# Linear attention feeding a gated feed-forward layer: q laid out transposed by the host, one piece per partition for k, v and w_in, and another order of the first batch's stages

## The chip, the cores and the metric

The kernel runs on one core of one Trainium2 chip. The metric is the device time of one execution in microseconds (us). A smaller time is better. Laying the inputs out on the host, before the launch, is not part of the time.

## What is computed

For each of 8 batches and 8 heads (sequence 576, head size 64) the kernel forms `kv = k^T v` (64 by 64), then `out = q kv`, divides each row of `out` by its root mean square and multiplies it by `g_norm`. The heads side by side give a token's 512 values, for 4608 tokens. A feed-forward layer follows:

```python
kv = np.einsum('bhsd,bhse->bhde', k, v)
out = np.einsum('bhsd,bhde->bhse', q, kv)
rms = np.sqrt(np.mean(out * out, axis=-1, keepdims=True) + 1e-06)
x = (out / rms * g_norm)            # heads side by side: 4608 tokens x 512
h = x @ w_in                        # 512 x 2048
g = h * (1.0 / (1.0 + np.exp(-h)))
return g @ w_out                    # 2048 x 512
```

All data are 32-bit. The weights arrive as 64-bit numbers in the program's view, two 32-bit words each, that the kernel turns into a 32-bit value itself.

## The kernel before, in words

**The feed-forward part.** Tokens are taken in 9 tiles (`t`) of 512, the 2048 hidden values in 16 blocks (`f`) of 128. One step is one `(t, f)`. Every product is made of three matmuls, since each factor is split into a rounded high part and the rest (low part): `products` (L503) writes 12 matmuls of 512 columns into a PSUM bank `hp`, `gate` (L512) makes `gh`, `gf` and `gl` of it, and `project` (L532), two steps later (`LAG`), adds 12 matmuls of 512 columns into four banks `acc`.

**The weights.** A block of `w_in` or `w_out` is loaded by `load_block` (L95) and prepared once, in the first tile: `bits` (L125) makes the 32-bit value on VectorE, five instructions for the first blocks and three for later ones, whose first two are `magnitude` (L115) on ScalarE and GpSimd; `split_block` (L163) rounds on ScalarE (L166) and subtracts on GpSimd (L167).

**Attention of batches 1 to 7.** Class `Pair` treats two heads at once (4 pairs per batch), spread over the steps of the feed-forward part by `plan` (L551): `mm_kv` (L246), `split_kv` (L253 to L257), `turn_q` (L261, a transposition of 32x32 blocks on VectorE), `split_q` (L266 and L267), `mm_out` in two halves (L277 to L279), then the norm and `to_tile` (L312, L313), which writes the tiles `xh` and `xl` that the products read. Here q is loaded in four DMAs per pair, in runs of 32 values (128 bytes), and k and v in two DMAs each.

**Attention of batch 0.** It has to be done before the first products. Class `FirstPair` loads q, k and v of a pair into buffers (`early`) that weights will need later. `turn_q` (L341) transposes q by TensorE, `copy_q` (L346) brings it back from PSUM on ScalarE (once on VectorE); `make_kv` (L352) and `copy_kv` (L359) give the two 64x64 blocks; `make_out` (L365) multiplies; `square` (L369) and `norm` (L442 to L448) make the norm on VectorE, with one square root on ScalarE (L446); `make_x` (L378) transposes the result, and `x_from` writes the x tile, for pairs 0 and 1 by ScalarE twice and GpSimd (L467 to L469), for pairs 2 and 3 by ScalarE and VectorE (L458, L459). Class `Rest` does the last 64 tokens of the batch for all pairs.

**What sets the order.** Nothing is scheduled by a planner: each engine executes its instructions in the order in which the Python code issues them, and waits in that order. `ORDER` (L26) is the order of the loads, all on SyncE's queue, where from the ninth DMA on each issue waits until the one eight places earlier has landed. Lines 630 to 689 are the first batch's stages; the loop from L700 on is the rest.

## Time and profile before

| what | value |
|---|---|
| three timed runs | 891.77, 892.54, 892.55 us; median 892.54 |
| the profiled execution | 893.95 us, span 892.1 us |
| TensorE (PE) busy | 871.0 us, 98% of the span |
| VectorE (DVE) busy | 337.7 us, 38% |
| ScalarE (ACT) busy | 307.5 us, 34% |
| GpSimd (POOL) busy | 176.8 us, 20% |
| DMA | 108,389 packets, 55.26 MB; 76,464 packets under 512 bytes |

The profiled execution took 893.95 us; the profile covers 892.1 us of it (the span), and 1.85 us lie around it. Times in the profile count from the span's start. An instruction's row has its start, its duration, its engine, line and operation, and in brackets how long the engine stood idle before it and what released it.

### The profile page before, as it was taken

The page shows a single profiled execution, that of the slowest core. Times are in us where ns is not written, and L with a number is a line of the kernel's source. Part 1 is how long each engine was busy: PE and PEld are TensorE (multiplying, and loading weights), DVE is VectorE, ACT ScalarE, POOL GpSimd, SP SyncE. Part 2 cuts the span into 40 slices and gives each one's busy share as a digit, 9 for nine tenths or more (in the row PEclk, how much of TensorE's full clock was granted, in tenths as well). Part 3 has the DMA queues.
Part 4 walks back from the last instruction along what each step waited for, and adds up shares of the span by engine and source line. Part 5 has one row for each costly group of instructions (what it writes and reads, how often), then busy time and mean ns, then how long its engine had stood idle before and what let it go on. Part 6 is the DMA issues. An engine that isn't in the chain of part 4 may idle for free.

```text
span 892.1 us, 11345 instructions
## 1 busy us (share of the span) xinstructions
PE 871.0 (98%) x4438; PEld 713.1 (80%) x4438; DVE 337.7 (38%) x617; ACT 307.5 (34%) x684; POOL 176.8 (20%) x172
## 2 busy tenths in 40 slices
PE   7879989999999999999999999999999999999998
PEld 6658868888888888888888888888888888888887
DVE  5888894233232423341433233332523141111111
ACT  4567634332343224322432243322432231112121
POOL 1489963101120002101210112010310020000000
PEclk9899989999999999999999999999999999999999
DMA  9869402310052004300431024100400010001001
GB/s 243 257 212 326 117 0 80 87 41 1 11 148 49 0 1 128 80 1 1 116 65 28 1 71 96 41 1 1 127 1 1 1 47 1 1 1 48 0 1 48
DMA packets 108389, 55.26 MB, mean 62 GB/s; under 512 B 76464, under 2 KB 101808, under 8 KB 108336
## 3 DMA queue, kind: packets, MB, share of 16 engines
q1 hardware_dynamic: 108336, 54.54, 22.5%
q8 instruction: 35, 0.57, 0.3%
q14 instruction: 18, 0.15, 0.1%
HBM read 45.09 MB, written 9.44 MB: 61 GB/s over the span
## 4 chain that ended last, share of the span: by engine, by line
PE 87%; DMA 3%; DVE 3%; POOL 3%; issue 2%; SPq 1%; ACT 0%; DVEq 0%; POOLq 0%
PE hp L507 41%; PE acc L537 40%; PE at L246 2%; DMA early_wo<-in_q 1%; DMA wi<-in_moe_w_in 1%; DMA wo<-in_moe_w_out 1%; POOL wi L167 1%; PE at L278 1%; PE at L279 1%; PE at L277 1%; POOL full L120 1%; PE at L537 1%; DMA kv<-in_k 1%; DVE m L476 1%; POOL wo L167 1%
## 5 line engine op out<-in xcount | busy, mean ns | idle before, releaser
L507 PE MATMUL hp<-xh,wi 128*128 128x512 f32 x1144 | 355.4, 392 | 2.1 <-POOL wi L167 2.1
L537 PE MATMUL acc<-wo,gh 128*128 128x512 f32 (+1 forms) x1152 | 355.3, 390 | 1.4 <-POOL wo L167 1.4
L518 DVE TENSOR_TENSOR gl<-gf,gh 128x512 fp32r<-128x512 f32 x128 | 88.6, 692 | 500.5 <-ACT gf L517 500.5
L507 PEld LDWEIGHTS hp<-xh,wi 128*128 128x128 f32 x1144 | 215.9, 189 | 46.0 <-POOL wi L167 3.2
L537 PEld LDWEIGHTS acc<-wo,gh 128*128 128x128 f32 x1152 | 214.8, 188 | 45.8 <-POOL wo L167 1.8
L507 PE MATMUL hp<-xl,wi 128*128 128x512 f32 x572 | 227.8, 398 | 3.5 <-ACT wi L166 3.5
L516 ACT ACTIVATE gh<-hp 128x512 fp32r<-128x512 f32 x143 | 85.5, 598 | 416.8 <-PE hp L507 416.6
L537 PE MATMUL acc<-wo,gl 128*128 128x512 f32 x576 | 222.5, 386 | 0.0
L507 PEld LDWEIGHTS hp<-xl,wi 128*128 128x128 f32 x572 | 108.0, 189 | 26.8 <-ACT wi L166 3.9
L537 PEld LDWEIGHTS acc<-wo,gl 128*128 128x128 f32 x576 | 108.2, 188 | 23.8
L313 POOL TENSOR_TENSOR xl<-o,xh 128x448 fp32r<-128x448 f32 (+7 forms) x56 | 53.2, 951 | 343.5 <-ACT xh L312 343.5
L517 ACT ACTIVATE gf<-hp 128x512 f32<-128x512 f32 x143 | 84.6, 592 | 0.0
L267 POOL TENSOR_TENSOR ql<-qT,qh 128x576 fp32r<-128x576 f32 x28 | 40.1, 1431 | 177.0 <-ACT qh L266 88.5
L283 ACT ACTIVATE sq<-at 128x288 f32<-128x288 f32 x56 | 23.2, 415 | 39.4 <-PE at L279 26.8
L253 ACT COPY kvm<-at 64x64 f32<-64x64 f32 x56 | 11.6, 207 | 59.4 <-PE at L246 59.1
L304 DVE SCALAR_TENSOR_TENSOR o<-o,gcol,yT 128x448 f32<-128x448 f32 (+7 forms) x56 | 31.2, 557 | 2.0
L246 PEld LDWEIGHTS at<-kv 128*64 128x64 f32 (+1 forms) x560 | 20.8, 136 | 12.0 <-issue 9.7
L246 PE MATMUL at<-kv 128*64 128x64 f32 (+1 forms) x560 | 26.5, 231 | 0.0
L312 ACT CAST xh<-o 128x448 fp32r<-128x448 f32 (+7 forms) x56 | 24.8, 442 | 5.0 <-DVE o L304 5.0
L297 DVE STREAM_TRANSPOSE yT<-y 128x448 f32<-128x448 f32 (+7 forms) x56 | 25.9, 463 | 0.0
L167 POOL TENSOR_TENSOR wi<-full,wi 128x512 fp32r<-128x512 f32 x16 | 21.4, 1334 | 21.2 <-ACT wi L166 21.2
L284 ACT COPY o<-at 128x288 f32<-128x288 f32 x56 | 22.7, 406 | 4.0 <-POOL xl L313 4.0
(104 smaller groups left out, 514.5 us busy)
## 6 DMA issues: line engine op xcount, KB each, us to landing
out<-ob SPq DMA_DIRECT2D x35, 256.0 KB, 2.1
wi<-in_moe_w_in SPq DMA_DIRECT2D x16, 512.0 KB, 6.4
wo<-in_moe_w_out SPq DMA_DIRECT2D x16, 512.0 KB, 11.1
qt<-in_q SPq DMA_DIRECT2D x112, 72.0 KB, 3.7
kv<-in_k SPq DMA_DIRECT2D x28, 256.0 KB, 3.1
kv<-in_v SPq DMA_DIRECT2D x28, 256.0 KB, 3.6
kv<-in_k SPq DMA_DIRECT2D x28, 32.0 KB
kv<-in_v SPq DMA_DIRECT2D x28, 32.0 KB
```

What stands on the lines that cost most here:

```text
L167: nc.gpsimd.tensor_tensor(out=w[:, 1, :], in0=full, in1=w[:, 0, :].bitcast(F32), op=ALU.subtract)
L246: nc.tensor.matmul(out=self.kv[h], lhsT=self.k[rows, c, :], rhs=self.v[rows, c, :], start=(r == 0), stop=(r == 4))
L267: nc.gpsimd.tensor_tensor(out=self.ql, in0=self.qT, in1=self.qh.bitcast(F32), op=ALU.subtract)
L297: nc.vector.transpose(out=self.yT.rearrange("p (j a) -> p j a", a=32), in_=y[:, a // 32:e // 32].unsqueeze(2).to_broadcast([P, (e - a) // ...
L304: nc.vector.scalar_tensor_tensor(out=self.o[:, a:e], in0=self.o[:, a:e], scalar=gcol, in1=self.yT, op0=ALU.mult, op1=ALU.mult)
L312: nc.scalar.copy(out=th[:, self.c, w], in_=self.o[:, a:e])
L313: nc.gpsimd.tensor_tensor(out=tl[:, self.c, w], in0=self.o[:, a:e], in1=th[:, self.c, w].bitcast(F32), op=ALU.subtract)
L507: nc.tensor.matmul(out=hp[:, :TN], lhsT=w[:, a, fs], rhs=x[:, c, :], start=(c == 0 and i == 0), stop=(c == NP - 1 and i == 2),)
L516: nc.scalar.activation(out=gh, in_=hp[:, :TN], func=AF.Silu)
L517: nc.scalar.activation(out=gf, in_=hp[:, :TN], func=AF.Silu)
L518: (nc.gpsimd if t == 0 else nc.vector).tensor_tensor(out=gl, in0=gf, in1=gh.bitcast(F32), op=ALU.subtract)
L537: nc.tensor.matmul(out=bank, lhsT=g[:, ns], rhs=w[:, a, cs], start=(f == 0 and i == 0), stop=(f == NF - 1 and i == 2))
```

## The change

- On the host, `lay_out` gives q as [batch, pair, 128 (head and its 64 values), 576 tokens], k and v as [batch, pair, 128 partitions, 576 values], and `w_in` as 16 blocks of [128 partitions, 512 values]. So each load of q, k, v or a block of `w_in` is one DMA with one contiguous piece per partition: 2,304 bytes for q, k and v, 4,096 for `w_in`.
- q is ready for the matmuls when it lands. The transpositions of q (L261 on VectorE, L341 and L399 on TensorE) and their copies (L346, L406) are gone. `q` itself takes the place of `qT`.
- `FirstPair` uses the `Pair` code for its load and for k^T v: 10 matmuls over 128 rows in place of 12 over 96, into an `h` bank of its own for each pair.
- The loads of the first batch come in another order, and `w_in`'s block 1 behind the third pair.
- The first batch's stages are in another order: `b1`'s conversion moves behind the norm of pair 1, `make_x` of pairs 0 and 1 moves forward, the first six products come in another order.
- In tile 0 the tokens keep their order, so the x tile of batch 0 is written along PSUM's order.

```diff
 ORDER = """
-    wi0 q0 kv0 wi1 q1 kv1 q2 kv2 q3 kv3 g wi2 qq wo0 wi3 wo1 wi4 wo2 b0 wi5 wo3 b1 wi6 wo4 wi7 wo5 b2
+    wi0 p0 g p1 p2 wi1 p3 wi2 wo0 wi3 wo1 wi4 wo2 b0 wi5 wo3 b1 wi6 wo4 wi7 wo5 b2
     wi8 wo6 wi9 wo7 b3 wi10 wo8 wi11 wo9 wi12 wo10 wi13 wo11 wi14 wo12 wi15 wo13 wo14 wo15
...
+        src = w_in.bitcast(I32)[f] if kind == "wi" else w_out.bitcast(I32)[f * P:(f + 1) * P, :]
+        nc.sync.dma_start(out=t.rearrange("p a b -> p (a b)"), in_=src)
...
+        def load(self, place=None):
+            self.k, self.v, self.q = (
+                place() if place else kvq.tile([P, S], F32, name=name, tag="kvq") for name in ("k", "v", "q")
+            )
+            for t, src in ((self.k, k), (self.v, v), (self.q, q)):
+                nc.sync.dma_start(out=t, in_=src[self.b, self.c])
...
-        def turn_q(self):
-            self.qT = tmp.tile([P, S], F32, name="qT", tag="tmp")
-            nc.vector.transpose(out=self.qT, in_=self.q)
...
-            nc.scalar.copy(out=self.qh, in_=self.qT)
-            nc.gpsimd.tensor_tensor(out=self.ql, in0=self.qT, in1=self.qh.bitcast(F32), op=ALU.subtract)
+            nc.scalar.copy(out=self.qh, in_=self.q)
+            nc.gpsimd.tensor_tensor(out=self.ql, in0=self.q, in1=self.qh.bitcast(F32), op=ALU.subtract)
...
         b0, b1, b2 = (bits("wi", f) for f in range(3))
-        p0.turn_q()
-        p0.copy_q([nc.scalar.copy] * 2)
+        run(b0)
         p0.make_kv()
         p0.copy_kv()
-        run(b0)
+        split("wi", 0)
         p0.make_out()
-        split("wi", 0)
-        run(b1)
-        p1.turn_q()
         p0.square()
-        p1.copy_q([nc.scalar.copy] * 2)
         p1.make_kv()
+        p1.copy_kv()
         norm(p0)
-        p1.copy_kv()
-        p2.turn_q()
         p1.make_out()
         p1.square()
-        p2.copy_q([nc.scalar.copy, nc.vector.tensor_copy])
+        nc.vector.tensor_scalar(out=gcol, in0=gcol, scalar1=float(D) ** 0.5, scalar2=None, op0=ALU.mult)
         p2.make_kv()
+        make_x(p0)
         p2.copy_kv()
         norm(p1)
-        nc.vector.tensor_scalar(out=gcol, in0=gcol, scalar1=float(D) ** 0.5, scalar2=None, op0=ALU.mult)
-        p3.turn_q()
         p2.make_out()
-        p3.copy_q([nc.scalar.copy] * 2)
         p2.square()
-        split("wi", 1)
+        run(b1)
         p3.make_kv()
+        make_x(p1)
         p3.copy_kv()
-        norm(p2, b2[:2])
-        make_x(p0)
+        norm(p2)
         p3.make_out()
         p3.square()
-        norm(p3, b2[2:3])
-        run(b2[3:])
-        make_x(p1)
+        split("wi", 1)
         make_x(p2)
+        norm(p3, b2[:2])
         warm = [h_bank(), acc_bank()]
-        products(warm[0], 0, 0, 0)
-        products(warm[1], 0, 1, 0)
+        for c in range(2):
+            for f in range(WARM):
+                products(warm[f], 0, f, c)
         make_x(p3)
+        run(b2[2:])
         split("wi", 2)
-        rest.turn_q()
-        rest.copy_q()
         for f in range(WARM):
-            products(warm[f], 0, f, 1)
+            products(warm[f], 0, f, 2)
         rest.make_out()
         rest.square()
...
-        for f in range(WARM):
-            products(warm[f], 0, f, 2)
```

How the instructions move is shown at three places. The first is VectorE in the first batch, before: the conversion of `w_in`'s block 1 (`wi_119`), the norm of pair 0 (`m_330`, `y_332`), and a copy of the transposed q.

```order
L136 TENSOR_SCALAR full<-wi_119 128x512
L139 TENSOR_SCALAR full<-full 128x512
L152 TENSOR_SCALAR full<-full 128x512
L155 SCALAR_TENSOR_TENSOR full<-wi_119,full 128x512
L158 SCALAR_TENSOR_TENSOR full<-wi_119,full 128x512
L442 TENSOR_REDUCE m_330<-sq 128x8
L443 TENSOR_SCALAR m_330<-m_330 128x8
L198 SCALAR_TENSOR_TENSOR u_331<-y_332 128x8
L199 TENSOR_TENSOR u_331<-u_331,m_330 128x8
L200 SCALAR_TENSOR_TENSOR y_332<-u_331,y_332 128x8
L448 TENSOR_TENSOR on<-at,y_332 128x512
L346 COPY qT<-hp 64x512
```

VectorE with the change, from behind the norm of pair 0 on: the norm of pair 1 (`m_319`, `y_321`) and then the conversion of block 1, there called `wi_133`.

```order
L560 TENSOR_SCALAR gcol<-gcol 128x1
L363 TENSOR_REDUCE m_319<-sq 128x8
L364 TENSOR_SCALAR m_319<-m_319 128x8
L189 SCALAR_TENSOR_TENSOR u_320<-y_321 128x8
L190 TENSOR_TENSOR u_320<-u_320,m_319 128x8
L191 SCALAR_TENSOR_TENSOR y_321<-u_320,y_321 128x8
L369 TENSOR_TENSOR on<-acc,y_321 128x512
L127 TENSOR_SCALAR full<-wi_133 128x512
L130 TENSOR_SCALAR full<-full 128x512
L143 TENSOR_SCALAR full<-full 128x512
L146 SCALAR_TENSOR_TENSOR full<-wi_133,full 128x512
L149 SCALAR_TENSOR_TENSOR full<-wi_133,full 128x512
```

Block 1's five instructions stood ahead of the norm of pair 0 and stand now behind that of pair 1.

The second place is ScalarE in the same stretch, before: from the square root of pair 0 (`y_332`) to the k^T v blocks of pair 3 (`kvm_94`).

```order
L446 ACTIVATE y_332<-m_330 128x8
L359 COPY kvm_92<-at 64x64 x2
L369 ACTIVATE sq<-acc 128x512
L346 COPY qT<-hp 64x512
L359 COPY kvm_93<-at 64x64 x2
L446 ACTIVATE y_379<-m_377 128x8
L346 COPY qT<-hp 64x512 x2
L369 ACTIVATE sq<-acc 128x512
L166 CAST wi_408<-full 128x512
L359 COPY kvm_94<-at 64x64 x2
```

ScalarE with the change, over the same stretch (square roots `y_279` of pair 0 and `y_321` of pair 1):

```order
L367 ACTIVATE y_279<-m_277 128x8
L307 ACTIVATE sq<-acc 128x512
L388 ACTIVATE xf<-at,gcol 128x512
L389 CAST xh_310<-xf 128x512
L224 COPY kvm_93<-hp 64x64 x2
L367 ACTIVATE y_321<-m_319 128x8
L307 ACTIVATE sq<-acc 128x512
L388 ACTIVATE xf<-acc,gcol 128x512
L389 CAST xh_310<-xf 128x512
L224 COPY kvm_94<-hp 64x64 x2
```

The copies of the transposed q are gone, and the two instructions that write the x tile of a pair (`xf`, `xh_310`) now stand ahead of the blocks of the pair two places on and of the next pair's square root.

The third place is ScalarE at the first pair of batch 1, in the loop, before (`kh` and `qh` are the high parts of k^T v and q):

```order
L516 ACTIVATE gh<-hp 128x512
L517 ACTIVATE gf<-hp 128x512
L253 COPY kvm_91<-at 64x64 x2
L256 CAST kh<-kvm_91 128x128
L266 CAST qh<-qT 128x576
L468 CAST xh_593<-xf 128x4x64
```

And with the change:

```order
L437 ACTIVATE gh<-hp 128x512
L438 ACTIVATE gf<-hp 128x512
L224 COPY kvm_91<-at 64x64 x2
L230 CAST kh<-kvm_91 128x128
L236 CAST qh<-q 128x576
L389 CAST xh_503<-xf 128x4x64
```

The order is the same; `qh` now reads the loaded q instead of VectorE's `qT`.

## Rows read from the trace of the kernel before

**Rows 1.** Stages: stretch, length, busy PE, PEld, DVE, ACT, POOL, PEclk, DMA share, GB/s

```profile
0.00:39.10 39.10, 30.53 (x231) 24.30 (x232) 26.25 (x56) 19.46 (x43) 9.22 (x17) 0.91 0.96 260
39.10:57.90 18.80, 13.57 (x74) 9.88 (x72) 18.00 (x23) 10.83 (x23) 14.41 (x14) 1.00 0.70 188
124.20:134.00 9.80, 5.76 (x14) 4.13 (x14) 9.38 (x15) 4.51 (x9) 7.92 (x7) 0.65 0.00 0
134.00:888.80 754.80, 754.80 (x3781) 620.72 (x3779) 226.40 (x440) 230.11 (x522) 88.42 (x81) 1.00 0.15 38
```

**Rows 2.** Chain of waits, 0 to 40 us: start, length, what

```profile
4.91 9.59 DMA early_wo<-in_q
14.51 8.85 DMA wi<-in_moe_w_in
...
38.14 0.44 DVE on L448
...
39.12 0.93 PE hp L507 x4
```

**Rows 3.** Stretches as in rows 1: first batch's loads, then loads mostly of `w_out`

```profile
18.00:20.00 2.00, 1.88 (x17) 1.77 (x16) 1.52 (x6) 1.77 (x6) 0.00 (x0) 1.00 1.15 237
...
88.00:90.00 2.00, 2.00 (x23) 1.47 (x21) 1.97 (x4) 0.76 (x3) 2.00 (x3) 1.00 1.04 408
```

**Rows 4.** Timeline of TensorE, first batch (records: two per matmul of 32-bit data)

```profile
8.49 1.55 PE L352 MATMUL at<-early_wo,early_wi 96*64 96x64 f32 x24 [1.03 <-DMA early_wo<-in_v]
10.56 2.07 PE L365 MATMUL at<-kvm,qT 128*128 128x128 f32 x8 [0.52 <-ACT kvm L359]
...
16.09 1.06 PE L365 MATMUL acc<-kvm,qT 128*128 128x128 f32 x8
...
26.67 0.66 PE L378 MATMUL acc<-ident,on 128*128 128x128 f32 x4 [3.18 <-DVE on L448]
...
29.20 1.09 PE L378 MATMUL acc<-ident,on 128*128 128x128 f32 x4
```

**Rows 5.** Timeline of ScalarE, first batch

```profile
15.31 0.43 ACT L359 COPY kvm<-at 64x64 f32<-64x64 f32 x2
...
22.92 0.69 ACT L467 ACTIVATE xf<-at,gcol 128x512 f32<-128x512 f32 x1
23.64 0.62 ACT L468 CAST xh<-xf 128x512 fp32r<-128x512 f32 x1
```

**Rows 6.** Timeline of VectorE and GpSimd, first batch

```profile
4.66 0.43 DVE L136 TENSOR_SCALAR full<-wi 128x512 int32<-128x512 int32 x1 [4.66 <-DMA wi<-in_moe_w_in]
...
6.77 0.69 DVE L158 SCALAR_TENSOR_TENSOR full<-wi,full 128x512 int32<-128x512 int32 x1
...
11.23 1.75 POOL L167 TENSOR_TENSOR wi<-full,wi 128x512 fp32r<-128x512 f32 x1 [9.36 <-ACT wi L166]
11.89 1.64 DVE L158 SCALAR_TENSOR_TENSOR full<-wi,full 128x512 int32<-128x512 int32 x1
...
17.82 0.69 DVE L442 TENSOR_REDUCE m<-sq 128x8 f32<-128x512 f32 x1 [0.51 <-ACT sq L369]
...
19.65 0.69 DVE L448 TENSOR_TENSOR on<-acc,y 128x512 f32<-128x512 f32 x1
```

**Rows 7.** Timeline at the first pair of batch 1: ScalarE, GpSimd, TensorE

```profile
53.65 0.67 ACT L266 CAST qh<-qT 128x576 fp32r<-128x576 f32 x1 [1.71 <-DVE qT L261]
...
54.46 1.41 POOL L267 TENSOR_TENSOR ql<-qT,qh 128x576 fp32r<-128x576 f32 x1 [1.46 <-ACT qh L266]
...
55.92 0.40 PE L277 MATMUL at<-ql,kh 128*128 128x288 f32 x1 [2.27 <-POOL ql L267]
...
57.86 0.73 PE L507 MATMUL hp<-xh,wi 128*128 128x512 f32 x2 [1.04 <-POOL wi L167]
```

**Rows 8.** Timeline near the end of the first tile: VectorE, TensorE

```profile
108.32 3.55 DVE L476 COPY m<-sums 32x72 f32<-32x72 f32 x1
...
127.76 0.80 PE L507 MATMUL hp<-xl,wi 128*128 128x512 f32 x1 [3.48 <-ACT wi L166]
```

More of the change, by code (lines that the diff above doesn't have):

```diff
@@ L50, in linear_attention_rms_silu_ffn @@
     nc = tc.nc
-    B, H, S, D = q.shape
-    DM, FF = w_in.shape
-    P = 128
-    NP = H // 2
-    NF = FF // P
+    B, NP, P, S = q.shape
+    D = P // 2
+    DM = NP * P
+    NF = w_in.shape[0]
     TN = 512
@@ L73, in linear_attention_rms_silu_ffn @@
     ps_at = ctx.enter_context(tc.tile_pool(name="ps_at", bufs=1, space=PSUM))
-    kvm = [const.tile([P, P], F32, name=f"kvm{i}") for i in range(H // 2)]
+    kvm = [const.tile([P, P], F32, name=f"kvm{i}") for i in range(NP)]
     for t in kvm:
@@ L84, in load_g @@
     def load_g():
-        for h in range(2):
+        for h in range(P // D):
             nc.sync.dma_start(out=gcol[h * D:(h + 1) * D, :], in_=g_norm.rearrange("(d o) -> d o", o=1))
@@ L253, in split_kv @@
                 nc.scalar.copy(out=self.kvm[d, d], in_=self.kv[h])
+        def split_kv(self):
+            self.copy_kv()
             self.kh = kvp.tile([P, P], F32R, name="kh")
@@ L364, in make_out @@
                 w = slice(r * P, (r + 1) * P)
-                nc.tensor.matmul(out=self.ps[:, w], lhsT=self.qT[:, w], rhs=self.kvm, start=True, stop=True)
+                nc.tensor.matmul(out=self.ps[:, w], lhsT=self.q[:, w], rhs=self.kvm, start=True, stop=True)
         def square(self):
@@ L381, in to_tile @@
             return x_from(
-                [y[:, self.c, :].rearrange("d (p r) -> d p r", r=4) for y in x_tiles(0)],
-                self.ps.rearrange("d (r p) -> d p r", r=4), fast,
+                [y[:, self.c, :].rearrange("d (r p) -> d r p", r=4) for y in x_tiles(0)],
+                self.ps.rearrange("d (r p) -> d r p", r=4), fast,
             )
@@ L410, in make_out @@
                 rows, w = slice(64 * (c % 2), 64 * (c % 2) + 64), slice(c // 2 * P, (c // 2 + 1) * P)
-                nc.tensor.matmul(out=self.o[rows, w], lhsT=self.qT[:, c, :], rhs=kvm[c], start=True, stop=True)
+                nc.tensor.matmul(out=self.o[rows, w], lhsT=first[c].q[:, TN:S], rhs=kvm[c], start=True, stop=True)
         def square(self):
@@ L429, in linear_attention_rms_silu_ffn, with early @@
     slots = [f"{kind}{f}" for f in range(NF - 1, 0, -1) for kind in ("wo", "wi")]
-    def early(shape):
+    def early():
         name = slots.pop(0)
-        return weights.tile(shape, F32, name=f"early_{name}", tag=name)
+        return weights.tile([P, S], F32, name=f"early_{name}", tag=name)
     def token_norm(o, ps, sq):
```

115 lines of the change are left out of this document (26 added, 89 removed).

## Prediction, made before the changed kernel was run

> **What bounds the kernel now.** I read the stages first. From 134 us to the last matmul at 888.8 us TensorE is busy in every microsecond, at a granted clock of 1.00, while the other engines are busy less than a third of it [rows 1]. There only a change in TensorE's own work could move the end, and a pair of batches 1 to 7 issues the same matmuls with the change (its k^T v has 10 before and after). So all that can be won or lost lies before 134 us, in three places: the 39.1 us before the third block's products begin, the 18.8 us behind that in which TensorE works 13.57, and the stop at 124 us, with a clock of 0.65 over its 9.8 us [rows 1].
>
> Next the chain of waits for the start. It names two loads, 9.59 us for a q and 8.85 us for block 2 of w_in; behind them comes VectorE up to the norm of the last 64 tokens (38.14), and TensorE's steady products at 39.12 [rows 2]. That number, 39.12, is what the first part of the sum is held against.
>
> **The change, part by part.**
>
> *Loads.* Behind w_in's block 0 (landed 4.66 [rows 6]) came 0.85 MB of q, k and v of pair 0, landed just before 8.49 [rows 4]: 0.224 MB per us. Now k and v come first, 0.59 MB. At the old rate they land at 7.3. The new pieces are 2,304 and 4,096 bytes where q, k, v and w_in had 1,024 to 1,536; the row with such small pieces moved 237 GB/s, the one mostly of 4,096-byte pieces 408 [rows 3]. I take the middle, 322, a factor of 1.36, since 2,304 lies between: block 0 at about 4.1, v at 6.0. Bounds: 5.2 (408) and 7.3. The Trainium skill ("DMA: Bandwidth & Descriptors", Specifications) gives 512 bytes as the smallest transfer for full line rate. By it the old pieces would be fast enough already and the gain of rate would be none; the two rows differ by a factor of 1.7, which speaks against it.
>
> *The first batch.* Without the wait for loads it is a chain of small steps over four engines. I follow it with the durations of before, about 0.05 us for each handover.
> - k^T v of pair 0: 10 matmuls instead of 12, 1.55 x 10/12 = 1.3 [rows 4], to 7.3; its copy 0.5 [rows 5], 7.8; the four matmuls with q, 1.9 at the early, slow rate (10.56, pipelined end taken off; later 1.06 [rows 4]), 9.7. Pair 1 the same: 1.3, 0.5, 1.9, to 13.4.
> - On TensorE k^T v of pair 2 (0.9) and the transposition of pair 0's result (0.65 [rows 4]): 14.95. Now ScalarE's new order matters: the two writes of the x tile, 0.69 + 0.62 [rows 5], stand ahead of pair 2's blocks (0.43) and of pair 1's square root (0.2), which is done at 16.95. VectorE has been waiting for that since about 15.
> - A norm takes 2.5 from reduction to result (17.82 to 20.34 [rows 6]), its part behind the square root 1.35. GpSimd's subtraction for pair 0's x tile runs from 16.35 on, and VectorE's steps on SBUF data are held while GpSimd works: a step of 0.69 took 1.64 beside one [rows 6]. I count 0.7 here: 19.05.
> - Block 1's conversion, which hid in the wait for loads before, now lies bare: 2.8 (4.66 to 7.46 [rows 6]) and a hold of 0.95 by pair 1's subtraction: 22.8. This is the dearest move of the change.
> - Norm of pair 2, 2.5: 25.3. Its transposition, high part and low part, 0.75 + 0.7 + 0.75: 27.5. Reduction of pair 3 and two steps of block 2, 0.9 + 0.9, then 1.35: 30.65.
> - TensorE stands still here about 2.8 us before pair 2's transposition. Before, a stop of 3.18 us was followed by the lower of its clock's two levels, 1.2 instead of 2.4 GHz: the same four transpositions took 0.66 and then 1.09 [rows 4]. So pair 3's take 1.2 with the handover, then 0.7 and 0.75: 33.3.
> - Block 2's last three steps 1.9, w_out's block 0 first three 1.3 with a hold of 0.9, the last tokens' reduction 0.6, two steps 1.4, the norm's end 1.1, the last transposition 0.6: 41.1.
>
> That is 2.0 later than 39.12. What was removed (40 transpositions of q on TensorE, nine copies on ScalarE, one on VectorE) had stood in the shadow of the loads, and gives little. Bounds: with v at 5.2, pair 1 at full speed (-0.85), no half speed later (-0.45) and no holds (-2.55) it is 36.5, 2.6 earlier than before; with v at 7.3 and one more hold of 0.95, 43.4, 4.3 later.
>
> *From the first products to 57.86.* VectorE is busy 18.0 of 18.8 us here [rows 1] and the others follow it, so the 2.0 goes through. TensorE will have stood 3 to 5 us before the last transposition and then runs at half speed again; its waits in this stretch, 18.8 - 13.57 = 5.2 [rows 1], cover what that costs: four products take 0.93 at full speed [rows 2], so a block of twelve costs 2.8 more at half of it. At the first pair of batch 1, ScalarE waited 1.71 for the transposition of q, GpSimd 1.46 for ScalarE, TensorE 2.27 for GpSimd, and then 1.04 more for the block that GpSimd does next [rows 7]. With q ready, GpSimd goes on at once: its 1.46 are gained, and all that follows begins 1.46 earlier. Bounds: 0 (another engine late by as much) to 1.71.
>
> *58 us to the end.* TensorE is the bound, so the sum is carried on. The 27 other transpositions on VectorE, the removed DMAs (five fewer per pair) and SyncE's time lie beside it and count nothing; only if VectorE or the loads ended last there would they count. q's buffer is now free only behind GpSimd's subtraction instead of VectorE's transposition; SyncE waits there with the weights' loads behind it, but saves three issues in return, and these blocks are used 10 us later. The stop at 124 us comes from VectorE: a copy of 72 columns held 3.55 us, then TensorE waits 3.48 [rows 8]. Nothing of the change lies in that stretch; I count 0, bounds -6.9 (of its 9.8 us 4.0 are idle, and the 5.76 busy hold one block of twelve products, 2.8 at full speed [rows 1]) and +3 (the hold doubled).
>
> *Sum.* +2.0 - 1.46 = +0.5. The profiled execution (893.95, span 892.1) would be 894.5; it lies 1.4 above the median of the runs, 892.54, which becomes **893.0**. About 0.2%, 1.8 us, is what a measurement of this kernel can tell from no change. The forecast is no difference that can be told.
>
> **The rivals.**
> - *The loads were the bound of the start* (faster, 0.20). The chain of waits says so [rows 2]. Block 2 landed at 23.36 and would land near 18.2 at 1.36 times the rate: 5.1 earlier, and with 1.46 that gives 886.0; if half of it survives, 888.5. Against it: block 2 is now needed only at 28 us, and the small steps fill the time.
> - *GpSimd holds VectorE more often* (slower, 0.24). Before, most SBUF-only steps of VectorE in the first batch ran while GpSimd had nothing to do, since it waited for loads; now five subtractions fall between them. I count three holds, 2.55. If the other two also meet a conversion or a norm, 0.95 each [rows 6], the time is 893.0 + 1.9 = 894.9. It decides from the moment that GpSimd's subtraction begins before VectorE's step, by a few tenths.
> - *The rate of the loads doesn't change* (0.08). Then v lands at 7.3, 1.3 later, and the time is 894.3. The Trainium skill's page "DMA: Bandwidth & Descriptors" (Specifications) would make it so.
> - *The stop at 124 us changes* (0.08). Its mechanism is a race of VectorE's copies with GpSimd's row of instructions, and all instructions before it shift a little. Without wait and slow clock 893.0 - 6.9 = 886.1, with a doubled hold 896.
>
> **How the numbers follow.** The forecast has 0.40, with a range of its own of 890.9 to 895.3 (the sum with 2.1 less or 2.3 more, about half of the way to the start's lower end and all of the way to its upper one). The range that should hold the time 8 times in 10 reaches to half of the first rival and all of the second with some of its tail: 888.6 to 897.0. Faster by over 0.2%: first rival 0.19, the stop 0.06, low end of the forecast 0.04: 0.29. Slower: second rival 0.21, third 0.03, the stop 0.01, high end of the forecast 0.05: 0.30. Within: 0.41.
>
> **What would show it.** In the changed profile v of pair 0 should be in by 6, the loads should run above 300 GB/s in the first 15 us, and VectorE should idle a few times for ScalarE's square roots, about 2 us before pair 1's. Block 1's conversion should begin near 19 and the block of 12 products at 41. At the first pair of batch 1 GpSimd's idle before its subtraction for q should be gone. From 134 us on TensorE should be as busy as before. The prediction is wrong if the 12 products begin before 38 or behind 43, if TensorE waits anywhere behind 134 us, or if the stop at 124 us differs by more than 2 us.

## The result: 0.36% slower, inside the range, and where the time went

The changed kernel took 895.92 us (median of six runs, 894.72 to 896.14), the kernel before 892.54 (median of six, 891.77 to 893.04). The ratio is 1.0036, with a 95% interval of 1.0023 to 1.0049. By the forecast's bound of 0.2% that is slower. The forecast of 893.0 us, no difference that can be told, was 2.9 us short. The range of 888.6 to 897.0 holds the result; the forecast's own, narrower one of 890.9 to 895.3 does not.

The profiled executions are 893.95 us before and 895.82 after, 1.87 apart. The medians are 3.38 apart: the profiled execution before lay 1.41 above its median, the one after 0.10 below. The two traces can account for the 1.87 alone; the rest is that the profiled execution before was a long one, and why it was isn't known.

Stages of the changed kernel (stretch, length, then busy PE, PEld, DVE, ACT, POOL, then PEclk, DMA share, GB/s), beside [rows 1]:

```profile
0.00:41.80 41.80, 27.36 (x174) 22.09 (x175) 23.77 (x55) 14.87 (x34) 8.05 (x17) 0.86 0.80 303
41.80:59.30 17.50, 15.70 (x75) 12.00 (x73) 16.81 (x21) 10.81 (x24) 14.57 (x14) 0.85 0.16 48
59.30:123.00 63.70, 62.46 (x328) 51.05 (x329) 53.04 (x78) 41.56 (x88) 55.60 (x56) 1.00 0.51 192
123.00:135.00 12.00, 7.67 (x27) 5.62 (x26) 11.45 (x19) 4.40 (x9) 7.34 (x6) 0.89 0.01 2
135.00:891.00 756.00, 755.95 (x3784) 621.67 (x3782) 215.05 (x418) 230.65 (x523) 90.22 (x83) 1.00 0.12 38
```

From 135 us on TensorE is busy throughout, as before; only its start is later. Ahead of that the first batch is longer (41.8 us instead of 39.1 by these stages), the next stage shorter by 1.3, and between 59 and 123 us TensorE now misses 1.24 us, where it missed none.

The loads did what the change is made for. In the stretch of [rows 3]:

```profile
18.00:20.00 2.00, 1.41 (x14) 1.29 (x16) 1.10 (x3) 0.95 (x5) 1.26 (x1) 0.93 1.01 397
```

It moves 397 GB/s instead of 237. The chain of waits no longer holds a load after the first (start, length, what):

```profile
1.63 4.76 DMA early_wi<-in_v
6.53 1.56 PE hp L217 x20
...
18.56 0.22 ACT y L367
18.80 0.78 DVE u L189
20.08 0.69 DVE on L369
20.77 0.34 DVE full L127
...
40.94 0.42 DVE on L369
```

The two loads of 9.59 and 8.85 us that led this chain before [rows 2] are gone from it. Yet the norm of the last 64 tokens, the last step of the first batch on VectorE (L369 here), begins at 40.94 us; before it began at 38.14 [rows 2]. The chain is now TensorE, ScalarE, VectorE in turn. TensorE in the first batch, beside [rows 4]:

```profile
6.53 1.53 PE L217 MATMUL hp<-early_wi,early_wo 128*64 128x64 f32 x20 [1.68 <-DMA early_wi<-in_v]
8.59 2.07 PE L303 MATMUL at<-kvm,early_wo 128*128 128x128 f32 x8 [0.52 <-ACT kvm L224]
10.59 1.53 PE L217 MATMUL hp<-early_wo,early_wi 128*64 128x64 f32 x20
12.65 2.07 PE L303 MATMUL acc<-kvm,early_wi 128*128 128x128 f32 x8 [0.52 <-ACT kvm L224]
...
24.05 2.08 PE L303 MATMUL acc<-kvm,early_wi 128*128 128x128 f32 x8 [1.80 <-ACT kvm L224]
...
41.51 0.66 PE L345 MATMUL at<-ident,on 128*128 128x128 f32 x2 [5.00 <-DVE on L369]
41.82 0.78 PE L428 MATMUL hp<-xl,wi 128*128 128x512 f32 x1
```

The last row is the first of the 12 products of the third block. Before, it was this row; the 39.12 of [rows 2] is where the transposition ahead of it ends.

```profile
38.88 0.48 PE L507 MATMUL hp<-xl,wi 128*128 128x512 f32 x1
```

In the first batch k^T v takes 1.53 and the products with q 2.07 for two pairs in a row; before, only the first pair's products with q took that long, the second's 1.06 [rows 4]. And VectorE, beside [rows 6]:

```profile
18.80 0.77 DVE L189 SCALAR_TENSOR_TENSOR u<-y 128x8 f32<-128x8 f32 x1 [2.53 <-ACT y L367]
...
20.69 0.42 DVE L127 TENSOR_SCALAR full<-wi 128x512 int32<-128x512 int32 x1
...
22.79 0.69 DVE L149 SCALAR_TENSOR_TENSOR full<-wi,full 128x512 int32<-128x512 int32 x1
```

It waits 2.53 us for pair 1's square root and then converts block 1 from 20.69 to 23.48, with nothing in that stretch to hide it. These are the two costs that the prediction named.

At the first pair of batch 1, beside [rows 7], and just behind it (ScalarE, GpSimd, TensorE):

```profile
54.65 0.67 ACT L236 CAST qh<-q 128x576 fp32r<-128x576 f32 x1
64.16 0.68 ACT L110 ACTIVATE full<-wo 128x512 f32<-128x512 f32 x1 [2.19 <-POOL wi L158]
...
55.76 1.49 POOL L237 TENSOR_TENSOR ql<-q,qh 128x576 fp32r<-128x576 f32 x1
...
57.31 0.40 PE L247 MATMUL at<-ql,kh 128*128 128x288 f32 x1 [0.76 <-DVE conv L146]
59.24 0.73 PE L428 MATMUL hp<-xh,wi 128*128 128x512 f32 x2 [1.04 <-POOL wi L158]
66.44 0.95 PE L217 MATMUL at<-v,k 128*64 128x64 f32 x20 [1.24 <-ACT o L254]
```

GpSimd's idle of 1.46 before its subtraction for q is gone, and TensorE waits 0.76 instead of 2.27. From the norm of the last 64 tokens to the products behind the wait it was 57.86 - 38.14 = 19.72 us, and is 59.24 - 40.94 = 18.30: 1.42 gained, where 1.46 was predicted. Then comes what was not predicted: ScalarE waits 2.19 us for GpSimd at 64 us, and TensorE 1.24 us for ScalarE at 66. The stop, beside [rows 8]:

```profile
130.49 0.50 PE L428 MATMUL hp<-xl,wi 128*128 128x512 f32 x1 [3.48 <-ACT wi L157]
...
138.82 0.39 PE L428 MATMUL hp<-xl,wi 128*128 128x512 f32 x1
```

It ends 89.55 us after that norm; before, 127.76 - 38.14 = 89.62. So the 1.42 are gone again. The block of products after it starts at 138.82; before, it was this row:

```profile
136.72 0.39 PE L507 MATMUL hp<-xl,wi 128*128 128x512 f32 x1
```

Sum: +2.80 at the norm, -1.42, +1.35 by the end of the stop, -0.63 in the products behind the stop (half clock for a shorter time: 8.33 us, instead of 8.96, from the end of the stop to the next block): +2.10. TensorE's last matmul is at 890.67 instead of 888.56, +2.11.

### The profile page after: what moved, and what is told of

Same layout as the page of the kernel before. It is cut to its first block, busy times and chain, and to the rows that moved or that the text cites. A ratio compares the mean times of both kernels' runs of the same rounds, so it can differ in the third digit from the quotient of the medians.

```text
span 894.0 us, 10971 instructions
## 1 busy us (share of the span) xinstructions
PE 869.1 (97%) x4382; PEld 712.4 (80%) x4382; DVE 320.1 (36%) x588; ACT 302.7 (34%) x675; POOL 175.8 (20%) x172
## 4 chain that ended last, share of the span: by engine, by line
PE 86%; DVE 5%; POOL 4%; issue 2%; ACT 1%; DMA 1%; SPq 0%; DVEq 0%; POOLq 0%; ACTq 0%
PE hp L428 40%; PE acc L458 40%; PE at L217 2%; POOL wi L158 1%; POOL full L111 1%; POOL gl L439 1%; PE at L248 1%; PE at L249 1%; PE at L247 1%; PE at L458 1%; DVE m L397 1%; DVE full L149 1%; DMA early_wi<-in_v 1%; PE hp L217 1%; DVE full L130 0%
## 5 line engine op out<-in xcount | busy, mean ns | idle before, releaser
L237 POOL TENSOR_TENSOR ql<-q,qh 128x576 fp32r<-128x576 f32 x28 | 40.1, 1432 | 176.3 <-ACT qh L236 172.2
L274 DVE SCALAR_TENSOR_TENSOR o<-o,gcol,yT 128x448 f32<-128x448 f32 (+7 forms) x56 | 33.8, 604 | 2.0
L217 PEld LDWEIGHTS at<-v,k 128*64 128x64 f32 (+1 forms) x560 | 20.8, 136 | 13.3 <-issue 9.7
L217 PE MATMUL at<-v,k 128*64 128x64 f32 (+1 forms) x560 | 26.5, 231 | 1.2 <-ACT o L254 1.2
```

The lines of the kernel that those rows point to most:

```text
L217: nc.tensor.matmul(out=self.kv[h], lhsT=self.k[rows, c, :], rhs=self.v[rows, c, :], start=(r == 0), stop=(r == 4))
L237: nc.gpsimd.tensor_tensor(out=self.ql, in0=self.q, in1=self.qh.bitcast(F32), op=ALU.subtract)
L274: nc.vector.scalar_tensor_tensor(out=self.o[:, a:e], in0=self.o[:, a:e], scalar=gcol, in1=self.yT, op0=ALU.mult, op1=ALU.mult)
```

## The experiments

One table first, for the numbers that the text returns to. "v" is the start of the first k^T v on TensorE, which waits for v of pair 0; "norm" the start of the last 64 tokens' norm on VectorE; "stop" the end of TensorE's stop; "last" the start of TensorE's last matmul, all in the profiled execution, in us. The ratio is to the kernel before, on the same chip, with its 95% interval.

| kernel | v | norm | norm - v | stop | stop - norm | last | ratio |
|---|---|---|---|---|---|---|---|
| before | 8.49 | 38.14 | 29.65 | 127.76 | 89.62 | 888.56 | 1 |
| changed | 6.53 | 40.94 | 34.41 | 130.49 | 89.55 | 890.67 | 1.0036 (1.0023 to 1.0049) |
| changed, again | 7.53 | 41.98 | 34.45 | 131.52 | 89.54 | 892.08 | 1.0028 (1.0017 to 1.0040) |
| unused buffer | 7.44 | 39.25 | 31.81 | 128.77 | 89.52 | 889.65 | 1.0036 (1.0024 to 1.0048) |
| old order | 7.12 | 36.46 | 29.34 | 126.21 | 89.75 | 887.37 | 0.9979 (0.9970 to 0.9989) |
| block 1 early | 7.02 | 39.45 | 32.43 | 129.00 | 89.55 | 889.89 | 1.0049 (1.0033 to 1.0065) |
| x tile later | 6.97 | 38.31 | 31.34 | 128.09 | 89.78 | 889.47 | 1.0018 (1.0005 to 1.0030) |
| both back | 6.63 | 35.93 | 29.30 | 125.75 | 89.82 | 886.99 | 0.9987 (0.9979 to 0.9996) |
| changed, filled | 7.37 | 39.21 | 31.84 | 128.76 | 89.55 | 889.27 | 0.9991 (0.9979 to 1.0002) |
| old order, nine | 6.66 | 35.48 | 28.82 | 125.38 | 89.90 | 886.55 | 0.9967 (0.9954 to 0.9979) |
| old order, nine, start filled | 6.83 | 34.59 | 27.76 | 122.93 | 88.34 | 882.89 | 0.9972 (0.9954 to 0.9989) |
| old order, nine, step filled | 7.95 | 36.75 | 28.80 | 125.10 | 88.35 | 885.57 | 0.9977 (0.9961 to 0.9993) |
| old order, nine, all filled | 7.72 | 36.40 | 28.68 | 124.72 | 88.32 | 885.06 | 0.9968 (0.9956 to 0.9980) |
| changed, nine | 6.84 | 39.25 | 32.41 | 127.60 | 88.35 | 887.66 | 1.0029 (1.0007 to 1.0051) |

Two questions were open. Is it the new order of the first batch that makes the norm late, or TensorE's half speed there? And who takes back the 1.42 us behind 58 us: ScalarE's wait for a buffer, or VectorE, if it sets the pace of the first tile in any case?

### The changed kernel with the old order

```diff
-    wi0 p0 g p1 p2 wi1 p3 wi2 wo0 wi3 wo1 wi4 wo2 b0 wi5 wo3 b1 wi6 wo4 wi7 wo5 b2
+    wi0 p0 wi1 p1 p2 p3 g wi2 wo0 wi3 wo1 wi4 wo2 b0 wi5 wo3 b1 wi6 wo4 wi7 wo5 b2
...
-        run(b0)
         p0.make_kv()
         p0.copy_kv()
-        split("wi", 0)
+        run(b0)
         p0.make_out()
+        split("wi", 0)
+        run(b1)
         p0.square()
         p1.make_kv()
-        p1.copy_kv()
         norm(p0)
+        p1.copy_kv()
...
-        make_x(p0)
         p2.copy_kv()
         norm(p1)
...
```

and so on to the first products: the sequence of the kernel before, without `turn_q` and `copy_q`.

> The new layout alone: the changed kernel with the order of loads and of the first batch's stages that the kernel before had, without the transpositions of q. Theory A (the new order costs: block 1's conversion lies bare, and the writes of the x tile stand ahead of pair 1's square root): the norm of the last 64 tokens, at 40.94 us with the change and at 38.14 before, comes at 36.5 to 38.5, and the time is 891.0 to 893.5. Theory B (the order costs nothing; TensorE is slower at the start because it lost the transpositions of q that kept it busy): the norm stays within 0.7 of 40.94, and the time is 895.2 or more.

The norm came at 36.46 and the time is 891.94 (before, beside it, 893.06): Theory A, with the norm 0.04 us below its lower end. TensorE was no faster here than in the changed kernel (1.53 and 2.07 for the first pair, 2.08 for the second), so its half speed is not what separates the two orders. The second pair's row:

```profile
14.72 2.08 PE L303 MATMUL acc<-kvm,early_wi 128*128 128x128 f32 x8 [2.01 <-ACT kvm L224]
```

The new layout with the old order beats the kernel before by 0.21%; the new order costs more than the layout brings. The gain of the layout is small for a reason that the table shows: the norm comes 29.34 us after v instead of 29.65, so 1.37 of its 1.68 us are the earlier v, 7.12 instead of 8.49. The transpositions of q and their copies that it removes show as no more than the other 0.31. The prediction had said that they give little; but here the second pair's products with q took 2.08 us and before 1.06 [rows 4], so the 0.31 is what is left after that loss, and not the price of the transpositions alone.

### One move undone at a time, and both

Block 1's load and conversion early:

```diff
-    wi0 p0 g p1 p2 wi1 p3 wi2 wo0 wi3 wo1 wi4 wo2 b0 wi5 wo3 b1 wi6 wo4 wi7 wo5 b2
+    wi0 p0 wi1 g p1 p2 p3 wi2 wo0 wi3 wo1 wi4 wo2 b0 wi5 wo3 b1 wi6 wo4 wi7 wo5 b2
...
         p0.make_out()
+        run(b1)
         p0.square()
...
-        run(b1)
         p3.make_kv()
```

> The changed kernel with block 1 of w_in loaded behind pair 0 and converted ahead of the norm of pair 0, while VectorE waits; nothing else moved. Theory A (the 2.8 us of that conversion lie bare on VectorE and go through to the end): the norm of the last 64 tokens comes at 38.2 to 38.8 instead of 40.94, and the time is 893.2 to 893.7. Theory B (pair 2's norm would wait for something else, its square or its square root): the norm moves by under 0.8 and the time is above 895.0. A third outcome is that the loads of pairs 1 and 2, now behind 0.5 MB more, come too late: then TensorE waits for a DMA before 15 us.

The writes of the x tile behind the next pair's norm:

```diff
         p2.make_kv()
-        make_x(p0)
         p2.copy_kv()
         norm(p1)
+        make_x(p0)
...
         p3.make_kv()
-        make_x(p1)
         p3.copy_kv()
         norm(p2)
+        make_x(p1)
```

> The changed kernel with the writes of the x tile of pairs 0 and 1 moved behind the norm of the next pair; nothing else moved. Theory A (they hold back pair 1's square root): VectorE's wait of 2.53 us before 18.8 us falls to 0.8 or less, the norm of the last 64 tokens comes at 38.9 to 39.4 instead of 40.94, and the time is 894.0 to 894.5. Theory B (the two writes cost the same wherever they stand; they then hold back pair 2): the norm moves by under 0.6 and the time stays above 895.3.

Neither came out as its Theory A had it. With block 1 early the norm is 32.43 us after v instead of 34.41, and yet the time is not better at all (1.0049). VectorE had the conversion out of its way and then waited for pair 2's square root (timeline of VectorE, block 1 early):

```profile
18.04 0.77 DVE L189 SCALAR_TENSOR_TENSOR u<-y 128x8 f32<-128x8 f32 x1 [1.82 <-ACT y L367]
...
23.21 0.77 DVE L189 SCALAR_TENSOR_TENSOR u<-y 128x8 f32<-128x8 f32 x1 [2.40 <-ACT y L367]
```

The 2.40 are ScalarE's two writes of pair 1's x tile, which stand ahead of that root. With the x tile later it is the other way round (VectorE, x tile later): the roots are in time, and block 1's conversion lies between the norms, one step of it held beside GpSimd, 1.38 instead of 0.43:

```profile
17.35 0.42 DVE L127 TENSOR_SCALAR full<-wi 128x512 int32<-128x512 int32 x1
17.80 1.38 DVE L130 TENSOR_SCALAR full<-full 128x512 f32<-128x512 f32 x1
...
21.01 0.68 DVE L363 TENSOR_REDUCE m<-sq 128x8 f32<-128x512 f32 x1
```

So each of the two seems to fill the hole that taking away the other leaves. That was tried with both:

> The changed kernel with both moves undone together: block 1's load and conversion early, and the writes of the x tile of pairs 0 and 1 behind the next pair's norm. Theory A (these two are what the new order costs, and they add up; alone they brought 1.5 and 2.6 us at the norm of the last 64 tokens): the norm comes at 36.4 to 37.4, as with the whole old order (36.46), and the time is that of the old order, about 892. Theory B (they share what they win, since both shorten the same wait for pair 2): the norm comes at 37.9 or later, and the time is 893.5 or more.

The norm comes at 35.93, 29.30 us after v, as with the whole old order (29.34), and the time is 892.64 (before 893.68). Theory A holds for what the order costs: 34.41 - 29.30 = 5.1 us from v to the norm, at the same half speed of TensorE for the first two pairs (2.07 each; pair 3's products with q took 2.08 in the changed kernel and 1.16 here, but they are not on its chain of waits). That the two add up, as that theory also said, is not shown. From v to the norm the single runs gain 1.98 and 3.07, together 5.05, but they look better there than they are, since in both the clock rose by pair 1 (products with q 1.16 us); the next runs show what that alone is worth. In time the single runs stand at 1.0049 and 1.0018, the two together at 0.9987, where the changed kernel has 1.0028 beside it.

### TensorE's gaps filled in the changed kernel, and the changed kernel again

```diff
-        keep_warm(6)
+        keep_warm(10)
...
             self.ps = self.ps or acc_bank()
+            fill(self.ps, FILL[self.c])
             for r in range(4):
...
-        at(last_jobs, 1, rest.make_x, lambda: moves.extend(rest.to_tile()), lambda: moves.pop(0)())
+        at(last_jobs, 1, lambda: fill(rest.x, 14), rest.make_x, lambda: moves.extend(rest.to_tile()), lambda: moves.pop(0)())
```

`fill(bank, n)` issues n matmuls of the identity by itself into the bank, `FILL` is (1, 1, 4, 4).

> The changed kernel with idle matmuls of 128 columns in TensorE's gaps of the first batch: 4 more at the start, 1 ahead of the products with q of pairs 0 and 1, 4 ahead of those of pairs 2 and 3, 14 ahead of the last transposition. Their results are written over. Theory A (without the transpositions of q TensorE stands still between the steps and works at half speed; k^T v takes 1.53 us instead of 0.92 and the products with q 2.07 instead of 1.06, four of them in a row ahead of pair 1's square root): the norm of the last 64 tokens comes 1.0 to 3.6 us earlier than 40.94, the 12 products of the third block take about 2.8 us instead of 5.2, and the time is 892.5 to 894.8. Theory B (TensorE's speed is hidden behind VectorE's chain): the norm moves by under 0.6, the time stays within 0.7 of the changed kernel's.

> The changed kernel once more, on the chip of these runs, so that the others have it beside them. Theory A (the difference of 3.4 us is the program's): 1.002 to 1.005 times the kernel before. Theory B (it was that chip or that hour): within 0.1% of it. The second profile also shows what varies from one execution to the next: if the landing of v of pair 0 (6.53 us) or the clock of the first 30 us moves, the norm of the last 64 tokens (40.94 us) moves with it.

On one chip the changed kernel took 896.43 us, the filled one 893.33, the kernel before 893.68: 1.0028 and 0.9991, with intervals that don't meet. The filled kernel reaches the norm 31.84 us after v, the changed one 34.45. So half speed does cost the changed kernel about 2.6 us at the norm: Theory A of the filled run, at the norm and in time. The fills of 14 missed their place: they write the bank that the norm reads, waited for VectorE like the transposition behind them, and the 12 products came later; from the norm to the end of the stop it took 89.55 us all the same.

The changed kernel again is slower than before by 0.28%, so the difference belongs to the program. Its second profile has v one microsecond later and the norm 1.04 later.

Without any fill, though, the clock can rise early too. Two other kernels here have the first batch of the changed kernel, instruction for instruction, "unused buffer" and "changed, nine" (below), and reach the norm 31.81 and 32.41 us after v. Their rows, pair 1's products with q, unused buffer first:

```profile
12.94 1.16 PE L304 MATMUL acc<-kvm,early_wi 128*128 128x128 f32 x8 [0.53 <-ACT kvm L224]
```

```profile
12.95 1.16 PE L303 MATMUL acc<-kvm,early_wi 128*128 128x128 f32 x8 [0.52 <-ACT kvm L224]
```

where the changed kernel had 2.07 both times. The Trainium skill ("TensorE: Matmul & The Clock Gate", What's actually happening) says that the number of slow matmuls at a kernel's start differs from one run of a kernel to the next. These four executions fit that, with 2.0 to 2.6 us between two of them and the other two at the norm, but don't prove it: both profiles of the changed kernel itself had the late rise. What speaks for chance, and against the two programs, is that their profiled executions lay 2.2 and 2.8 us under their own medians (894.80 for 897.04, 892.75 for 895.58), so the early rise was not the rule in them. Even with the early rise the new order's norm comes 2.5 to 3.1 us later after v than the 29.30 of both moves undone at half speed.

### Where the 1.42 us go: an unused buffer, and nine of them

All temporary tiles, q's split parts, VectorE's transposed squares and the magnitudes of weights (L110) among them, come from one ring of eight buffers. The transposed q was one of them.

```diff
         def split_q(self):
+            self.pad = tmp.tile([P, S], F32, name="pad", tag="tmp")
             self.qh = tmp.tile([P, S], F32R, name="qh", tag="tmp")
```

> The changed kernel with one more temporary buffer taken and never used in each pair of batches 1 to 7, where the transposed q stood before. Theory A (the temporary buffers go round in a ring of eight; without the transposed q, ScalarE's next magnitude at 64 us gets a buffer that GpSimd still has to read): ScalarE's wait of 2.19 us for GpSimd at 64 us is under 0.6, TensorE's wait of 1.24 us at 66 us is gone, the stop that began at 127.0 us begins at about 125.7, and the median of 895.9 becomes 894.6. Theory B (VectorE's late start of 2.8 us sets tile 0 anyway): the stop begins at 127.0 as before and the time stays at 895.9, whatever happens at 64 us.

Theory A fell as it was put. ScalarE's wait stood there unchanged:

```profile
62.45 0.68 ACT L110 ACTIVATE full<-wo 128x512 f32<-128x512 f32 x1 [2.19 <-POOL wi L158]
```

TensorE again waited 1.24 us behind it, and the stop came 89.52 us after the norm. Whether a buffer that is never written takes a place in the ring at all, the run doesn't tell. The trace of the kernel before does tell that the ring's order moved. There the same instruction of ScalarE waited 0.23 us for a matmul that reads q's low part (L277), and began before GpSimd's subtraction for this block of `w_in`, for whose end it waits in the changed kernel (ScalarE, GpSimd, before):

```profile
60.81 0.67 ACT L119 ACTIVATE full<-wo 128x512 f32<-128x512 f32 x1 [0.23 <-PE at L277]
...
61.44 1.30 POOL L167 TENSOR_TENSOR wi<-full,wi 128x512 fp32r<-128x512 f32 x1
```

So the wait is not only the pace of TensorE, 1.42 us ahead, running into an old limit. The other way to loosen the ring is to make it longer, first in the better order:

```diff
-    tmp = ctx.enter_context(tc.tile_pool(name="tmp", bufs=8))
+    tmp = ctx.enter_context(tc.tile_pool(name="tmp", bufs=9))
```

> The old order with the new layout, and nine temporary buffers in place of eight. Theory A (ScalarE's magnitude waits 2.15 us at 59.6 us for a buffer that GpSimd still has to read, because the ring is eight long and a pair now takes one buffer fewer): the wait is under 0.5, the stop that ended at 126.2 us ends 0.8 to 1.5 us earlier, and the time is 0.8 to 1.5 us under that of the old order with eight (891.9). Theory B (TensorE is late there in any case, the wait costs nothing): the stop ends within 0.4 of 126.2 and the time is within 0.5 of 891.9.

ScalarE's wait was gone, and the stop ended at 125.38, 0.83 us earlier; the time is 890.49, 1.45 under the old order with eight. By its own numbers that is Theory A. But the norm had come 0.98 earlier already, and from there the stop still ended after 89.90 us: measured from the norm nothing was gained, which is Theory B. Nor does the time decide it: beside the kernel before the two orders stand at 0.9967 and 0.9979, with intervals that overlap. What took the gain here was another thing, in the same place. TensorE, old order with nine buffers:

```profile
51.84 0.40 PE L247 MATMUL at<-ql,kh 128*128 128x288 f32 x1 [0.83 <-DVE conv L146]
...
53.76 1.14 PE L428 MATMUL hp<-xh,wi 128*128 128x512 f32 x2 [1.03 <-POOL wi L158]
54.70 0.63 PE L428 MATMUL hp<-xl,wi 128*128 128x512 f32 x1
55.12 1.06 PE L428 MATMUL hp<-xh,wi 128*128 128x512 f32 x2
```

Behind two short waits the products run at the lower of the clock's two levels, 1.2 instead of 2.4 GHz, 1.06 instead of 0.62 for two matmuls (granted clock 0.73 from 54 to 60 us). In the changed kernel the same two waits were followed by 0.63. Of the ten profiles with these two waits left unfilled, four show the fall (the old order with eight and with nine buffers, x tile later, both back) and six don't, so the waits alone don't decide it. So in one kernel the buffer takes the gain back, in the other the clock. If so, TensorE keeps it where both are away:

```diff
             self.ps = ps = at_bank()[:, :HS]
+            if self.b == 1 and self.c == 0 and half == 0:
+                fill(ps, 3)
...
+                    if g == FILLED:
+                        fill(hp, 4)
                     for c in range(NP):
                         products(hp, t, f, c)
```

(`FILLED` is 4, on the old order with nine buffers.)

> The old order with nine buffers, and 3 and 4 idle matmuls in the two waits of TensorE at the first pair of batch 1 (0.83 and 1.03 us at 51.8 and 53.8 us), behind which the 12 products ran at half the clock. In all kernels run so far the stop of TensorE ends 89.5 to 89.9 us after the norm of the last 64 tokens begins on VectorE, with or without the transposition of q. Theory A (TensorE gains the 1.46 us there and loses them at once, by half the clock or by ScalarE's wait for a buffer; with both away the gain stays): the products behind the waits take 0.62 per two matmuls, the stop ends 88.0 to 88.7 us after that norm, and the time is 0.8 to 1.6 us under the old order with nine buffers. Theory B (VectorE's and GpSimd's preparing of the weights sets the pace to the stop): the stop ends 89.3 to 90.0 after the norm, and only TensorE's idle time there is longer.

```profile
53.11 0.40 PE L250 MATMUL at<-ql,kh 128*128 128x288 f32 x1 [0.16 <-DVE conv L147]
...
55.05 0.73 PE L431 MATMUL hp<-xh,wi 128*128 128x512 f32 x2
55.62 0.40 PE L431 MATMUL hp<-xl,wi 128*128 128x512 f32 x1
55.85 0.62 PE L431 MATMUL hp<-xh,wi 128*128 128x512 f32 x2
```

The products run at full speed (granted clock 1.00 from 54 to 60 us), and the stop ends 88.35 us after the norm: Theory A in the profile, 1.55 earlier than without the fills. VectorE, which does the same work in both, does not set that stretch. That the fills kept the clock up is likely but not shown by these two profiles, since it also stayed up elsewhere without them. In time the run says nothing: 0.9977, with an interval of 0.16% either way, against 0.9967. Last, in the changed kernel itself, only the ninth buffer:

> The changed kernel with nine temporary buffers in place of eight, nothing else. Theory A (the 1.46 us that TensorE gains at the first pair of batch 1 are given back because ScalarE's magnitude, about 5 us after them, waits 2.2 us for a buffer of the ring that GpSimd still reads, and TensorE then 1.24 for ScalarE): both waits are gone and the stop ends 88.2 to 88.6 us after the norm of the last 64 tokens begins on VectorE, instead of 89.5 to 89.9, as long as the products behind 58 us run at 0.62 per two matmuls; the time is 1.0 to 1.5 us under the changed kernel's. Theory B (the changed kernel's VectorE sets the stop): the stop ends 89.5 or more after that norm though the products run at 0.62, and the time is the changed kernel's within 0.5. If the clock falls to half there, this run doesn't tell the two apart.

```profile
39.25 0.42 DVE L369 TENSOR_TENSOR on<-at,y 128x256 f32<-128x256 f32 x1
...
57.55 0.73 PE L428 MATMUL hp<-xh,wi 128*128 128x512 f32 x2 [1.03 <-POOL wi L158]
58.13 0.39 PE L428 MATMUL hp<-xl,wi 128*128 128x512 f32 x1
58.36 0.63 PE L428 MATMUL hp<-xh,wi 128*128 128x512 f32 x2
...
127.60 0.50 PE L428 MATMUL hp<-xl,wi 128*128 128x512 f32 x1 [3.63 <-ACT wi L157]
```

The clock stayed up, ScalarE's wait of 2.19 and TensorE's of 1.24 are gone, and the stop ends 88.35 us after the norm instead of 89.55: 1.2 us, TensorE's wait of 1.24. So the gain of the transposition that VectorE no longer makes is real, and in the changed kernel ScalarE's wait for a buffer of the ring gives it back. The ring's order moved with the change, as the rows above show; that it moved because the transposed q left the ring is argued, not shown: putting a buffer back, unused, didn't undo it. The timed runs of this kernel spread from 888.04 to 899.87 us, and their ratio, 1.0029 (1.0007 to 1.0051), doesn't tell 1.2 us from nothing.

### The old order with nine buffers and TensorE's start filled

```diff
-        keep_warm(6)
+        keep_warm(10)
...
+            fill(self.ps, FILL[self.c])
             for r in range(4):
...
-        at(last_jobs, 1, rest.make_x, lambda: moves.extend(rest.to_tile()), lambda: moves.pop(0)())
+        spare = []
+        at(last_jobs, 1, lambda: spare.append(h_bank()), lambda: fill(spare[0], 6), rest.make_x, lambda: moves.extend(rest.to_tile()), lambda: moves.pop(0)())
...
-                    hp = h_bank()
+                    hp = spare.pop() if spare else h_bank()
```

(`FILL` is (1, 3, 1, 2).)

> The old order with nine buffers, and idle matmuls of 128 columns in TensorE's gaps of the first batch: 4 more at the start, 1, 3, 1 and 2 ahead of the products with q, 6 ahead of the last transposition, written over later. Theory A (TensorE's half speed at the start delays this order too: the products with q of three pairs took 2.07 us each instead of 1.06): from the landing of v of pair 0 to the norm of the last 64 tokens on VectorE it takes 26.5 to 28.3 us instead of 28.8, and the time is 0.5 to 2.3 us under that of the old order with nine buffers. Theory B (in this order VectorE's chain covers it): 28.5 or more, and the time is the same within 0.5.

> Both fills together on the old order with nine buffers. If they act in different places the time is that order's less the sum of what each brings alone: 1.3 to 3.9 us under it by theories A of both, the same within 0.5 by theories B of both.

The start filled brought the norm to 27.76 us after v, Theory A in the profile by a microsecond but not in time, and its last matmul at 882.89 is the earliest of all; 1.56 of that is the clock that happened to stay up behind 52 us. With all fills norm - v is 28.68, so the gain at the start did not repeat. The times of the four kernels of this family, 0.9967, 0.9972, 0.9977 and 0.9968, can't be told apart, and whether the fills add up stays open. All four beat both kernels, by 0.2 to 0.3% the kernel before. The simplest of them is the old order with nine buffers.

## Why the prediction was right and wrong

**The start, forecast +2.0, measured +2.8 at the norm and +2.9 at the 12 products (41.82 for 38.88).** The forecast's mark was the end of the last transposition, 39.12 before; there it is 42.17, 1.1 us behind the forecast of 41.1. The mechanism held. The two moves that the prediction priced, block 1's conversion laid bare and the writes of the x tile ahead of pair 1's square root, are what the order costs: undone together they take 5.1 us off the way from v to the norm. The size was off early in the chain. v came in at 6.53, not 6.0. k^T v was put at 1.3 for pairs 0 and 1 and 0.9 for pair 2; all three took 1.53. With them pair 1's square root was done at 18.77 instead of 16.95. Later steps gave back 0.7 of these 1.8: the conversion of block 1 was not held by GpSimd (22.8 forecast, 23.48 measured, from a norm 1.7 late), and pair 3's transpositions ran at full speed (0.66, not 1.2). The second profile of the changed kernel had the norm another 1.04 later, behind a v that was 1.00 later. The rate assumed for the loads, 322 GB/s, was too low for most of them (397), but not for those that count: block 0 landed at 4.32, and the 0.59 MB of k and v behind it took 2.2 us more, 267 GB/s.

**The first pair of batch 1, forecast -1.46, measured -1.42, then lost.** The term was right where it was counted. The step that failed is "all that follows begins 1.46 earlier", and the zero from 58 us on. The lower bound had it, "another engine late by as much", but the prediction looked only at the engines of that wait and not at the ring of buffers that the removed step had drawn on. ScalarE's wait of 2.19 us, and TensorE's 1.24 behind it, are a wait for a buffer of that ring: the ninth one took both away.

**From 58 us to the end, forecast 0, measured +1.35 and -0.63.** The first is the step above. The second is the half clock behind the stop, which lasted a little less long. From 135 us on nothing waits, as forecast, and the stop did not change: TensorE waits 3.48 us in both.

**The sum.** +2.80 - 1.42 + 1.35 - 0.63 = +2.10 in TensorE's last matmul, against +0.5. The median moved by more, 3.4, since the profiled execution before was a long one; the forecast carried the difference over to the median as it stood. That the result lies in the range owes something to luck: the range reached up to 897.0 for the second rival and its tail, and that rival is not what happened. Of the prediction's signs three failed: v by 6 us (6.53), loads above 300 GB/s in the first 15 us (298), block 1's conversion near 19 (20.69).

**The rivals.** "The loads were the bound": no. With 397 GB/s instead of 237 the norm came later, and even in the old order the layout gained 1.68 us at the norm and not 5.1. The prediction's ground for it, that small steps would fill the time, is what the chain of waits shows. "GpSimd holds VectorE more often": no. There were three holds in the first batch, as counted, at 18.80, 24.11 and 37.08, of 2.4 us together where 2.55 was counted. "The rate doesn't change": no, it rose by 1.7, so [rows 3] were the better guide, and not the smallest piece of 512 bytes that the Trainium skill ("DMA: Bandwidth & Descriptors", Specifications) gives for full line rate. "The stop changes": no. The chance of 0.30 for slower was mostly given to the second rival; the time went by the forecast's own path, further along it, and by the buffer.

## What to carry to other kernels

A stage that waits for loads hides work; before its loads are made faster or its steps reordered, list what the wait covered, and put each exposed step where the next wait is; undoing one of two moves can show nothing where undoing both shows all. When a step is removed, follow the buffers as well as the engines: a ring that suited the old sequence can make another engine wait and give the gain back. And a gain at one wait is only worth what the next few microseconds leave of it; measure it from a fixed event before to a fixed event after, as norm to stop here, and compare the profiled execution with its own kernel's median before it is taken for the rule.

## What the runs showed of the hardware that was not expected

- TensorE ran at half speed at the start without the granted clock showing it. In the changed kernel k^T v took 1.53 us at 6.53 and 0.95 at 66.44, while the stretch around the first reads 1.00 (columns as in the stages above):

```profile
4.80:10.00 5.20, 3.00 (x27) 2.67 (x27) 2.23 (x4) 1.03 (x3) 0.74 (x1) 1.00 0.87 284
10.00:15.00 5.00, 4.48 (x38) 3.72 (x38) 2.11 (x7) 1.47 (x5) 0.53 (x1) 1.00 1.05 403
20.00:25.00 5.00, 3.20 (x28) 2.56 (x25) 4.75 (x8) 2.00 (x5) 1.25 (x1) 0.50 1.03 403
```

  There the durations of the rows are the measure, and not this column. From 20 to 25 us, where it reads 0.50, the two agree (k^T v of pair 3 took 1.53). In the unused-buffer kernel the column reads 0.89 and 0.78 in the first two stretches, lower than here, although TensorE was faster there: k^T v took 0.95 and 1.49, pair 1's products with q 1.16 (pair 0's 2.07, as here).
- The same sequence of instructions reached the norm 31.8 to 34.5 us after v in four executions of three kernels; the difference that the rows show is the clock.
- v of pair 0 was used between 6.53 and 7.95 us in the thirteen profiles with the new layout, though the first four loads of all of them are the same. In the two profiles of the changed kernel, 1.00 later at v was 1.04 later at the norm; so v alone can move the time by up to 1.4 us, 0.16%.
